# Loading a small vector to all 128 partitions by DMA instead of spreading it with a matrix product, and joining two runs of idle products

## The chip, the cores and the metric

The kernel runs on one core of one Trainium2 chip. The metric is the device time of one execution in microseconds (us). An execution is measured several times; most agree within 0.3%. "Span" below is the length of the profiled part of an execution, from the first to the last instruction of the program. In before it is about 1.8 us less than the time. Every run quoted here was classed as fast, and only such runs are compared.

## The reference, cut to what matters

Block-wise linear attention with a decay per head, followed by a gated feed-forward layer. Lambda is a vector of 8 values, one for each head, 32 bytes in all.

```python
# lam: [8] in 0.97..0.99; q, k, v: [4, 8, 768, 64]
Dmask = where(rel >= 0, lam ** rel, 0)            # inside a block
for b in range(nb):
    intra = (qb @ kb.T * Dmask) @ vb
    inter = (qb * lam ** (pos + 1)) @ kv_state
    out[b] = intra + inter
    kv_state = lam ** block * kv_state + (kb * lam ** (block - 1 - pos)).T @ vb
x = out as [3072, 512]
return (sigmoid(x @ w_gate) * (x @ w_val)) @ w_out
```

All powers of lambda are made on the chip. They are needed on every partition, so the 8 values have to get from one row in memory to 128 partitions.

Of the kernel before, what the change touches and what calls it, by code (L numbers as in the profile page):

```python
# [7 lines left out]
FP32 = mybir.dt.float32  # L8
BF16 = mybir.dt.bfloat16
AF = mybir.ActivationFunctionType  # L10
# [5 lines left out]
def kernel(  # L16
# [11 lines left out]
    nc = tc.nc  # L28

    B, H, S, D = q.shape  # L30
# [10 lines left out]
    const = ctx.enter_context(tc.tile_pool(name="const", bufs=1))  # L41
# [9 lines left out]
    ps_at = ctx.enter_context(tc.tile_pool(name="ps_at", bufs=5, space=bass.MemoryType.PSUM))  # L51
# [4 lines left out]


    lam_bc = const.tile([128, H], FP32, tag="lam_bc")
    lam1 = const.tile([1, H], FP32, tag="lam1")
    nc.sync.dma_start(out=lam1, in_=lam.partition_broadcast(1))  # L60

    WG = const.tile([128, NMT, DFF], BF16, tag="WG")
    WV = const.tile([128, NMT, DFF], BF16, tag="WV")
# [51 lines left out]
    jn = const.tile([128, 2], FP32, tag="jn")  # L115
    ip1 = const.tile([128, C], FP32, tag="ip1")
    tri = const.tile([128, C], FP32, tag="tri")
    ones = const.tile([1, 128], FP32, tag="ones")
    nc.vector.memset(zero, 0.0)
    nc.vector.memset(ones, 1.0)  # L120
    Sb = stp.tile([128, B, HP, D], BF16, tag="Sb", name="Sb")
    nc.vector.memset(ip1[:, 0:1], 1.0)
    w = 1
# [30 lines left out]
    def idle(n):  # L154
        for i in range(n):
            nc.tensor.matmul(wm, lhsT=zero[:, :C], rhs=zero, start=True, stop=True,
                             skip_group_check=True)

    idle(4)
    lamp = ps_at.tile([128, H], FP32, name="lamp", tag="ps")  # L160
    nc.tensor.matmul(lamp, lhsT=ones, rhs=lam1, start=True, stop=True)
    lnl = const.tile([128, H], FP32, tag="lnl")
    nc.scalar.activation(lnl, lamp, AF.Ln)
    lnp = const.tile([128, HP], FP32, tag="lnp")
    for u in range(2):
        us = slice(u * 64, (u + 1) * 64)
        nc.scalar.activation(lnp[us, :], lamp[us, u::2], AF.Ln)
    nc.scalar.copy(lam_bc, lamp)
    lamq0 = const.tile([128, HP, C], BF16, tag="lamq0")
    for hp in range(HP):  # L170
        nc.scalar.activation(lamq0[:, hp, :], ip1, AF.Exp, scale=lnp[:, hp:hp + 1])
# [6 lines left out]
    for u in range(2):  # L178
        us = slice(u * 64, (u + 1) * 64)
# [313 lines left out]
    load_gv(1, GW)  # L493
    load_gv(2, GW)

    idle(6)
    nc.vector.tensor_copy(Q[0][:, 0], q01[0])
    piece_tq0([0])
    make_mask(0)
# [198 lines left out]
```

## The kernel before: the parts that the change touches

The program is scheduled by hand: each engine's instructions are written in the order in which it is to execute them.

```python
lam_bc = const.tile([128, H], FP32, tag="lam_bc")
lam1 = const.tile([1, H], FP32, tag="lam1")
nc.sync.dma_start(out=lam1, in_=lam.partition_broadcast(1))      # 32 bytes, one partition
# ...
nc.scalar.dma_start(out=q01[0], ...)     # q of batch 0, f32, ScalarE's queue
nc.sync.dma_start(out=q01[1], ...)       # q of batch 1, f32, Sync's queue, behind lambda
# ... VectorE: zero, ones, ip1 (1..128), ident, tri, in about 20 small instructions
load(0, "k", 0, 2)                       # K of block 0, GpSimd's queue (casts f32 to bf16)
# ... the rest of q, v and the weights, GpSimd's queue

def idle(n):                             # products of zeros that nobody reads
    for i in range(n):
        nc.tensor.matmul(wm, lhsT=zero[:, :C], rhs=zero, ...)

idle(4)
lamp = ps_at.tile([128, H], FP32, name="lamp", tag="ps")
nc.tensor.matmul(lamp, lhsT=ones, rhs=lam1, start=True, stop=True)   # spread to 128 partitions
nc.scalar.activation(lnl, lamp, AF.Ln)
# ... Ln to lnp, copy to lam_bc; Exp to lamq0, pk, kds, dec;
#     between them ScalarE's cast of q01[1] to bf16
# ...
idle(6)
nc.vector.tensor_copy(Q[0][:, 0], q01[0])    # VectorE's cast of q of batch 0
piece_tq0([0])                               # first transposes on TensorE, q of batch 0
make_mask(0)
idle(1)
piece_tq0([1])                               # transposes of q of batch 1
piece_tk0(0)                                 # transposes of K, tile tk
# ... scores, masks, block 0's output, first products with the weights
make_lamq()                                  # VectorE, about 21 us: lp and lamq from lam_bc
# ... from about 25 us on: products with the weights, nearly without a gap
```

The idle products are there for the clock. In the trace of before TensorE runs at half rate up to 7.5 us: the transposes start 107 ns apart at 6.06 us and 56 ns apart at 7.93, an idle product lasts 634 ns before 7.2 us and 379 ns at 8.32, and the clock records have full rate from 7.72 us on.

## Time and profile before

| | before |
|---|---|
| time | 227.16 us median of 3 runs (227.02 to 227.65) |
| span of the profiled run | 225.7 us |
| TensorE busy | 217.9 us, 97% |
| K of block 0 landed | 7.82 us |
| first transposes of K | 7.86 us |
| steady products with the weights | from 25.9 us |

The page of the profile gives busy time by engine (us, share of the span, instructions) and the chain of work that ended last, as shares of the span. These are lines of the page of before:

```profile
PE 217.9 (97%) x1728; PEld 115.2 (51%) x1750; DVE 106.5 (47%) x194; ACT 79.1 (35%) x150; POOL 78.4 (35%) x77
...
PE 91%; DVE 3%; DMA 3%; issue 2%; ACT 1%; DVEq 0%; POOLq 0%
```

TensorE (PE) bounds the kernel as a whole. The change lies in the first 7 us, and there the chain is another. Below it stands in order of time for before, taken from the first 30 us: start, duration, what.

```profile
1.26 6.56 DMA kb<-in_k_dram
...
7.86 0.63 PE tk L242 x8
...
25.92 0.86 PE gp L419 x4
```

For 6.56 us the chain is one load, K's. Work that ends before 7.8 us has slack against it. The timeline of before shows that work: start, duration, engine, line of the program, operation, output and inputs, sizes, count, and in brackets the idle time before it with what ended that.

```profile
0.74 0.34 SPq L60 DMA_DIRECT2D lam<-in_lam_dram  x1
1.19 1.89 PE L156 MATMUL wm<-zero 128*128 128x512 bf16 x4 [1.19 <-DVE zero L119]
3.01 0.59 PE L161 MATMUL lamp<-lam,ones 1*128 1x8 f32 x2
...
3.64 0.18 ACT L163 ACTIVATE lnl<-lamp 128x8 f32<-128x8 f32 x1 [1.17 <-PE lamp L161]
4.25 1.28 ACT L171 ACTIVATE lamq<-ip,lnp 128x128 bf16<-128x128 f32 x4
5.47 0.41 DVE L497 CAST qb<-q0f 128x512 bf16<-128x512 f32 x1
5.63 0.60 ACT L174 CAST qb<-q1f 128x512 bf16<-128x512 f32 x1
6.06 0.63 PE L242 MATMUL tq<-ident,qb 128*128 128x128 bf16 x4
```

ScalarE (ACT) starts on lambda when the product lamp is there, works through lamq0 and then casts q of batch 1. VectorE (DVE) casts q of batch 0 at 5.47 us, and the first transposes follow at 6.06.

### The profile page before, as it was taken

How to read it: one execution, taken by the hardware profiler on the slowest of the kernel's cores; microseconds unless marked ns; L12 is line 12 of the kernel's file. 1: busy time of each engine (PE TensorE's matmuls, PEld its weight loads, DVE VectorE, ACT ScalarE, POOL GpSimd, SP SyncE). 2: the span in 40 equal slices, each digit the busy share in tenths (PEclk: the TensorE clock that was granted, in tenths of full speed). 3: DMA queues.
4: the chain of work that ended last, by engine and by line, in shares of the span. 5: the costliest groups of instructions: out<-in, count | busy, mean ns of one | idle time of the engine just before them, and what ended most of it. 6: DMA issues, size and time to landing. Idle time of an engine off the chain costs nothing.

```text
span 225.7 us, 4250 instructions
## 1 busy us (share of the span) xinstructions
PE 217.9 (97%) x1728; PEld 115.2 (51%) x1750; DVE 106.5 (47%) x194; ACT 79.1 (35%) x150; POOL 78.4 (35%) x77
## 2 busy tenths in 40 slices
PE   7789999999999999999999999999999999999994
PEld 2445454888864455444545444446444445444443
DVE  7798647586521622435742345742334840333300
ACT  5463234434422225333215333225333225333221
POOL 8987687973493007940005950000000000000000
PEclk9999999999999999999999999999999999999999
DMA  8999999999999991999521999921940012100022
GB/s 122 154 174 196 186 176 151 145 194 169 155 146 183 217 208 75 180 137 147 23 93 49 190 134 145 46 96 46 153 84 0 0 50 93 49 0 0 0 93 94
DMA packets 105749, 25.70 MB, mean 114 GB/s; under 512 B 95874, under 2 KB 102786, under 8 KB 105730
## 3 DMA queue, kind: packets, MB, share of 16 engines
q0 software_dynamic: 81264, 13.90, 94.6%
q1 hardware_dynamic: 23426, 11.28, 22.4%
q10 hardware_dynamic: 1040, 0.26, 0.5%
q8 instruction: 13, 0.21, 0.4%
q14 instruction: 6, 0.05, 0.1%
HBM read 28.31 MB, written 6.29 MB: 153 GB/s over the span
## 4 chain that ended last, share of the span: by engine, by line
PE 91%; DVE 3%; DMA 3%; issue 2%; ACT 1%; DVEq 0%; POOLq 0%
PE po L482 27%; PE gp L419 21%; PE vp L425 20%; PE gp L454 5%; PE vp L460 5%; PE sp L304 3%; PE gp L433 3%; PE op L316 3%; DMA kb<-in_k_dram 3%; PE op L328 1%; PE po L471 1%; PE cp L403 1%; DVE MT L206 1%; DVE lp L194 1%; DVE ht L446 1%
## 5 line engine op out<-in xcount | busy, mean ns | idle before, releaser
L428 DVE TENSOR_TENSOR ht<-sg,vp 128x512 bf16<-128x512 bf16 x54 | 37.2, 688 | 65.6 <-PE vp L425 60.4
L482 PE MATMUL po<-WO,ht 128*128 128x512 bf16 x266 | 61.3, 379 | 0.5
L419 PE MATMUL gp<-XT,WG 128*128 128x512 bf16 x211 | 55.0, 379 | 0.6 <-issue 0.2
L425 PE MATMUL vp<-XT,WV 128*128 128x512 bf16 x211 | 54.4, 379 | 0.0
L422 ACT ACTIVATE sg<-gp 128x512 bf16<-128x512 f32 x54 | 32.2, 597 | 59.3 <-PE gp L419 59.3
L482 PEld LDWEIGHTS <-ht 128*128 128x128 bf16 x276 | 26.2, 98 | 31.0
L425 PEld LDWEIGHTS <-WV 128*128 128x128 bf16 x216 | 21.1, 98 | 25.5
L419 PEld LDWEIGHTS <-WG 128*128 128x128 bf16 x216 | 20.8, 98 | 24.7
L485 ACT COPY ob<-po 128x512 f32<-128x512 f32 x23 | 13.5, 586 | 52.2 <-PE po L482 48.4
L208 DVE TENSOR_TENSOR MT<-sp,mask 128x512 bf16<-128x512 f32 x40 | 25.2, 683 | 9.3 <-PE sp L304 9.3
L386 POOL TENSOR_TENSOR sd<-Sb,dec 128x512 f32<-128x512 bf16 x8 | 8.1, 1036 | 42.7 <-DVE Sb L410 42.6
L454 PE MATMUL gp<-XT,WG 128*128 128x256 bf16 x96 | 14.4, 273 | 0.0
L460 PE MATMUL vp<-XT,WV 128*128 128x256 bf16 x96 | 14.4, 273 | 0.0
L464 DVE TENSOR_TENSOR ht<-sg,vp 128x256 bf16<-128x256 bf16 x24 | 10.0, 420 | 8.6 <-PE vp L460 8.6
L457 ACT ACTIVATE sg<-gp 128x256 bf16<-128x256 f32 x24 | 9.2, 384 | 13.0 <-PE gp L454 11.8
L92 POOL DMA_DIRECT2D vb<-in_v_dram x10 | 12.8, 1285 | 0.8 <-DMA WG<-in_moe_w_gate_dram 0.6
L377 POOL TENSOR_TENSOR kd<-kb,kds 128x1024 bf16<-128x1024 bf16 x6 | 11.3, 1905 | 4.5 <-DMA kb<-in_k_dram 4.5
L410 DVE TENSOR_TENSOR Sb<-cp,sd 128x512 bf16<-128x512 f32 x8 | 5.2, 686 | 15.5 <-PE cp L403 15.5
L343 ACT CAST XT<-op 128x512 bf16<-128x512 f32 x19 | 9.9, 598 | 2.1 <-PE op L316 2.0
L454 PEld LDWEIGHTS <-WG 128*128 128x128 bf16 x96 | 9.2, 98 | 1.7 <-issue 0.2
L460 PEld LDWEIGHTS <-WV 128*128 128x128 bf16 x96 | 9.4, 98 | 1.1
L78 POOL DMA_DIRECT2D qb<-in_q_dram x8 | 9.4, 1183 | 0.0
(84 smaller groups left out, 162.9 us busy)
## 6 DMA issues: line engine op xcount, KB each, us to landing
out_dram<-ob SPq DMA_DIRECT2D x21, 256.0 KB, 2.3
kb<-in_k_dram POOLq DMA_DIRECT2D x10, 256.0 KB, 11.4
qb<-in_q_dram POOLq DMA_DIRECT2D x8, 256.0 KB, 9.8
vb<-in_v_dram POOLq DMA_DIRECT2D x4, 512.0 KB, 14.9
WO<-in_moe_w_out_dram POOLq DMA_DIRECT2D x3, 512.0 KB, 9.0
WG<-in_moe_w_gate_dram POOLq DMA_DIRECT2D x5, 256.0 KB, 8.3
WV<-in_moe_w_val_dram POOLq DMA_DIRECT2D x5, 256.0 KB, 8.5
qb<-in_q_dram POOLq DMA_DIRECT2D x6, 128.0 KB, 8.6
```

Source lines behind the costliest of these rows:

```text
L92: nc.gpsimd.dma_start(out=lst[n][:, b0:b1], in_=src[b0:b1, :, sl, :].rearrange("b h s d -> s (b h) d"))
L208: nc.vector.tensor_tensor(out=out.rearrange("p (e x) c -> p e x c", e=2), in0=x.rearrange("p (e x) c -> p e x c", e=2), in1=mask.rearrange ...
L377: nc.gpsimd.tensor_tensor(out=KD[n][:, e], in0=K[n][:, e], in1=kds[:, e::2].unsqueeze(1).unsqueeze(3).to_broadcast([128, B, HP, D]), op=AL ...
L419: nc.tensor.matmul(gp, lhsT=WG[:, mt, fs], rhs=x[:, mt, :], start=(mt == 0), stop=(mt == NMT - 1))
L422: nc.scalar.activation(sg, gp, AF.Sigmoid)
L425: nc.tensor.matmul(vp, lhsT=WV[:, mt, fs], rhs=x[:, mt, :], start=(mt == 0), stop=(mt == NMT - 1))
L428: nc.vector.tensor_mul(HT[n, ft], sg, vp)
L454: nc.tensor.matmul(gp[:, cs], lhsT=WG[:, mt, fs], rhs=x[:, mt, cs], start=(mt == 0), stop=(mt == NMT - 1))
L460: nc.tensor.matmul(vp[:, cs], lhsT=WV[:, mt, fs], rhs=x[:, mt, cs], start=(mt == 0), stop=(mt == NMT - 1))
L464: nc.vector.tensor_mul(HT[n, ft][:, cs], sg[:, cs], vp[:, cs])
L482: nc.tensor.matmul(po, lhsT=HT[n, ft][:, tt * 128:(tt + 1) * 128], rhs=WO[:, ft, :], start=(ft == 0), stop=(ft == NFT - 1))
L485: nc.scalar.copy(ob, po)
```

## The change

The intent: the DMA writes lambda to all 128 partitions itself, so the product, its two operands and a copy go away, ScalarE need not wait for TensorE, and the idle products run without a break up to the first transpose.

```diff
     lam_bc = const.tile([128, H], FP32, tag="lam_bc")
-    lam1 = const.tile([1, H], FP32, tag="lam1")
-    nc.sync.dma_start(out=lam1, in_=lam.partition_broadcast(1))
+    nc.sync.dma_start(out=lam_bc, in_=lam.partition_broadcast(128))
 ...
-    ones = const.tile([1, 128], FP32, tag="ones")
     nc.vector.memset(zero, 0.0)
-    nc.vector.memset(ones, 1.0)
 ...
-    idle(4)
-    lamp = ps_at.tile([128, H], FP32, name="lamp", tag="ps")
-    nc.tensor.matmul(lamp, lhsT=ones, rhs=lam1, start=True, stop=True)
-    nc.scalar.activation(lnl, lamp, AF.Ln)
+    nc.scalar.activation(lnl, lam_bc, AF.Ln)
 ...
-        nc.scalar.activation(lnp[us, :], lamp[us, u::2], AF.Ln)
-    nc.scalar.copy(lam_bc, lamp)
+        nc.scalar.activation(lnp[us, :], lam_bc[us, u::2], AF.Ln)
 ...
-    idle(6)
+    idle(10)
     nc.vector.tensor_copy(Q[0][:, 0], q01[0])
```

## The prediction

> **What bounds the kernel now.** TensorE: the page's busy table gives PE 217.9 us of a 225.7 us span, and the chain that ended last is 91% PE. The change touches only the first 7 us. There the chain in order of time is not PE but the load of K for block 0: 6.56 us of "DMA kb" from 1.26, landed at 7.82; the transposes tk start at 7.86, then KS copies, scores and masks follow. Whatever ends before 7.8 us has slack.
>
> **What the change does.**
> - Lambda. Before, one 32-byte packet filled one partition, four idle products ran from 1.19 us, and the PE product lamp (two passes, 3.01 to 3.6) spread it; ScalarE's first Ln started at 3.64 (waits: on lamp). After, the load itself writes 128 partitions. In the DMA view of narrow windows Sync's two packets ran at 1.5 to 1.8 us, before those of q0f began at 1.83, so I expect lambda landed by 2.3 to 3.0 us. Ln can start at 2.6 to 3.1, behind the table load (ends 2.47): 0.5 to 1.0 us earlier. ScalarE's lamq0 needs ip1, which VectorE finishes at 3.93, so it moves only from 4.25 to about 3.9; the lam_bc copy (0.17 us) goes. ScalarE gains about 0.35 us.
> - VectorE. One memset goes, about 0.05 us. It stays busy until the q0 cast at 5.47 to 5.88, which releases the first transpose, so this stays at 5.9 to 6.1.
> - TensorE. Ten idle products in one run, 0.427 us from start to start: 1.19 to about 5.5, instead of ending at 6.1 with a 0.5 us pause for lamp. A gap of about 0.4 us appears before the first transpose.
> - DMA. 127 more packets. At 2.5 to 3.0 us the 16 engines moved 551 packets, so 127 cost about 0.12 us, partly hidden in idle time before 2.5 us. K's landing may move by 0 to 0.12 us, the only term on the critical path.
>
> **Clock.** Idle products last 634 ns before 7.2 us and 379 ns at 8.32, so TensorE reached full speed between, just as K landed. [...]
>
> **Sum.** Lambda path -0.35 us, off the chain; K's landing +0.1 us at most[...]. Predicted 227.1 us, 226.4 to 227.9 in 8 of 10. Faster by over 2%: 0.01; within 2%: 0.98; slower by over 2%: 0.01.
>
> **What would show it.** Ln waits for lambda's DMA and starts before 3.2 us; lamq0 ends near 5.2; ten idle products without a hole; first transpose within 0.15 us of 6.06; K landing within 0.15 us of 7.82; from tk on, the same timeline shifted by under 0.2 us.
>
> **What would make it wrong.** Lambda's packets queued behind q0f's, landing after 4.5 us, so that the second transposes pass 7.86; small packets delaying K by more than estimated[...].

The sum came to 227.1 us, with 226.4 to 227.9 as its range: the time of before, lambda's path off the chain, and at most 0.1 us for K's landing. It had a further term, for the clock.

## The result, and the profile after

| | before | after |
|---|---|---|
| time, median of 6 runs | 227.14 us (226.73 to 227.65) | 227.13 us (226.66 to 227.86) |
| ratio, 95% interval | | 0.9999 (0.9975 to 1.0023) |
| span of the profiled run | 225.7 us | 225.3 us |
| K landed | 7.82 us | 7.34 us |

A ratio here is the mean time of one kernel's fast runs over the mean of the other's fast runs of the same rounds, so it is not quite the ratio of the medians beside it.

The time did not change. The profile inside did. The same places in the timeline of after:

```profile
0.74 0.41 SPq L59 DMA_DIRECT2D lam_bc<-in_lam_dram  x1
1.19 3.84 PE L153 MATMUL wm<-zero 128*128 128x512 bf16 x10 [1.19 <-DVE ip L119]
3.84 0.21 ACT L157 ACTIVATE lnl<-lam_bc 128x8 f32<-128x8 f32 x1 [1.33 <-DMA lam_bc<-in_lam_dram]
4.39 1.28 ACT L164 ACTIVATE lamq<-ip,lnp 128x128 bf16<-128x128 f32 x4
4.97 0.76 DVE L490 CAST qb<-q0f 128x512 bf16<-128x512 f32 x1
5.79 0.40 PE L235 MATMUL tq<-ident,qb 128*128 128x128 bf16 x4 [0.76 <-DVE qb L490]
6.04 0.62 ACT L167 CAST qb<-q1f 128x512 bf16<-128x512 f32 x1 [0.19 <-DMA q1f<-in_q_dram]
6.71 0.40 PE L235 MATMUL tq<-ident,qb 128*128 128x128 bf16 x4 [0.31 <-ACT qb L167]
7.39 0.62 PE L235 MATMUL tk<-ident,kb 128*128 128x128 bf16 x8 [0.27 <-DMA kb<-in_k_dram]
```

Lambda came later, not earlier. ScalarE waited 1.33 us for the load and began Ln at 3.84 us, against 3.64 with the product. It then waited 0.19 us for q1f and cast it at 6.04 instead of 5.63 us. The second transposes waited for that cast, and K's transposes waited only 0.27 us more for K. So in this execution the change used up most of the slack.

Two lines of the DMA view of after, for 2.0 to 2.5 us, show how the loads were held up: queue, packets, MB, share of 16 engines. Queue q1 is Sync's (lambda, then q1f), q10 is ScalarE's (q0f).

```profile
q10 hardware_dynamic: 28, 0.01, 6.3%
q1 hardware_dynamic: 35, 0.00, 3.2%
```

In before the same half microsecond had this:

```profile
q10 hardware_dynamic: 287, 0.07, 63.1%
```

The packet records of the trace of after have lambda's 128 packets from 1.8 to 3.5 us, 13 ns apart (1.72 us over 128). Until q0f's packets began beside them at 2.34 us the 16 engines were nearly idle (3.1% busy from 1.8 to 2.34 us). In before, q0f's 1024 packets of 256 bytes ran from 1.84 to 3.36 us, 1.5 ns apart; in after they ran from 2.34 to 4.38, 2.0 ns apart.

The chain of after in order of time, beside that of before:

```profile
1.26 6.08 DMA kb<-in_k_dram
...
7.39 0.63 PE tk L235 x8
...
20.66 0.41 DVE lp L183
...
25.69 0.86 PE gp L412 x4
```

K's transposes are 0.47 us earlier (7.39 against 7.86), but the steady products only 0.23 us (25.69 against 25.92). Three questions follow. Was K's earlier landing due to the change? Where did the rest of that lead go? And is the equal time one of no effects, or of effects that cancel?

The runs answer a part of the third. In the 30 runs of after, e2, e3, e4 and e10 the time is 2.08 to 2.22 us above the span; in the 88 listed runs of before and of the other kernels it is 1.72 to 1.85. The traces have it behind the last instruction: the last semaphore update comes 2.26 us after the end of the span in after and 1.90 in before. So the changed kernel pays 0.37 us more after its own work is done, in every run, and the six spans of after are 225.0 us on average, about 0.4 less than in before (225.4, estimated as its mean time less 1.78). The equal time is these two together. What lengthens the closing was not tested: e1 has the load without it, and e7, e9 and e11 have the load and the joined idle run without it.

### The profile page after: what moved, and what is told of

Read it like the earlier page. It is cut to its first block, busy times and chain, and to the rows that moved or that the text cites. A ratio compares the mean times of both kernels' runs of the same rounds, so it can differ in the third digit from the quotient of the medians.

```text
span 225.3 us, 4243 instructions
## 1 busy us (share of the span) xinstructions
PE 216.0 (96%) x1726; PEld 114.3 (51%) x1748; DVE 106.8 (47%) x193; ACT 79.2 (35%) x149; POOL 78.5 (35%) x77
## 4 chain that ended last, share of the span: by engine, by line
PE 91%; DVE 3%; DMA 3%; issue 2%; ACT 1%; DVEq 0%; POOLq 0%
PE po L475 27%; PE gp L412 21%; PE vp L418 20%; PE gp L447 5%; PE vp L453 5%; PE sp L297 3%; PE gp L426 3%; PE op L309 3%; DMA kb<-in_k_dram 3%; PE op L321 1%; PE po L464 1%; PE cp L396 1%; DVE MT L199 1%; DVE lp L187 1%; DVE ht L439 1%
```

## The experiments

Theory A: everything in the changed part ends before K lands, so the change is worth nothing, and the differences between the two profiles are scatter. Theory B: the load costs 0.4 us or more and the unbroken idle run wins it back through the clock. Theories C and D, on K's landing, came later. Twelve kernels were run, in four calls; kernels of one call share a chip and the runs of before.

### e1_load_only: the load alone

The change without the joined idle run; the product stays as a dummy that waits for no load.

```diff
-    nc.sync.dma_start(out=lam1, in_=lam.partition_broadcast(1))
+    nc.sync.dma_start(out=lam_bc, in_=lam.partition_broadcast(128))
-    nc.tensor.matmul(lamp, lhsT=ones, rhs=lam1, start=True, stop=True)
+    nc.tensor.matmul(lamp, lhsT=ones, rhs=ones[:, :H], start=True, stop=True)
     # Ln reads lam_bc; the copy to lam_bc goes; idle(4) and idle(6) stay
```

> The load of lambda to 128 partitions alone: the idle products stay in two runs of 4 and 6, and the PE product lamp stays between them as a dummy (ones times ones) that waits for no load and that nobody reads. Theory A (slack): everything in the changed part ends before K lands, both halves of the change are worth nothing, ratio to before 0.998 to 1.002. Theory B (two effects cancel): the 128 packets delay the loads by 0.4 us or more and the unbroken idle run wins it back through an earlier clock; then this kernel, which has only the cost, is 0.4 us or more slower than before (ratio 1.002 or more), and its idle products are still at half rate (634 ns) at 6 us.

Measured: 226.82 us, ratio 0.9978 (0.9950 to 1.0006). Theory B fails: the kernel with only the supposed cost was not slower. K's transposes were at 7.40 us, as in after, and full rate came at 5.4 us by the clock records, so neither of theory B's signs was there.

### e2_after_again: the changed kernel, once more

> The changed kernel unaltered, for a second profile and a narrower interval. Theory A: ratio 0.999 to 1.001; lambda's Ln again at 3.6 to 4.0 us and q0's last packets again about 1 us later than in the first profile of before, since those follow from the number of packets; K's landing anywhere from 7.3 to 7.9 us, since I take the 0.48 us between the two first profiles for scatter. Theory B: K lands at 7.3 to 7.4 again and full clock comes at about 4.2 us again.

Measured: 226.89 us, ratio 0.9981 (0.9956 to 1.0005), which is e1's: the two forms of the idle run cannot be told apart by time. Theory A's 0.999 to 1.001 was missed by the point, not by the interval. Ln was at 3.85 us and the cast of q1 at 6.02, as in the first profile of after. Full clock came at about 7.2 us here by the clock records, against 4.3 in the first profile of after: it changes from execution to execution. Both intervals include 1. The spans tell more: 224.5 to 224.8 us here, 225.5 on average in the 11 runs of before beside it, a lead of 0.8 us of which 0.37 goes in the closing.

K landed at 7.30 us, but its transposes did not wait for it. At half rate the transposes of q still ran, and the chain leads back through them to VectorE's cast of q0, not to K:

```profile
6.83 0.48 PE tq L235 x4
...
7.35 0.64 PE tk L235 x8
```

So in this execution of the changed kernel, and likewise in e3's, the slack was gone. In the second profile of before (before_again below), with K at 7.21 us, the chain leads through the idle products too. How much slack there is depends on when K lands and on the clock before that.

### e3_no_idle_run: no idle run at all

```diff
-    idle(10)
```

> The changed kernel without the run of ten idle products before the first transpose; the later single ones stay. Theory A and B agree that the array is then at half rate when K lands: tk's 8 transposes take about 1.0 us instead of 0.62, scores and first products twice as long[...]. I expect +0.6 to +2 us (ratio 1.003 to 1.009). If it is not slower (below 1.001), the clock before 12 us is worth nothing here and no part of theory B about the clock can hold.

Measured: 227.24 us, ratio 0.9997 (0.9973 to 1.0022). The chain in order of time:

```profile
7.34 1.05 PE tk L235 x8
...
20.03 5.30 PE gp L426 x24
25.33 0.86 PE gp L412 x4
```

K's transposes took 1.05 us instead of 0.63 as expected, but the rest of the forecast missed: the scores at 8.90 us already ran at full rate (8 products in 0.44 us), and the steady products came 0.24 us after e2's (25.33 against 25.09). I had expected 0.6 to 2 us; how long the half rate would last was not shown. The idle run was worth about 0.4 us here (0.9997 against 0.9981), with intervals of 0.5 us and more on each ratio.

### e4_lambda_x4: four times the load

```diff
+    for i in range(3):
+        lamx = const.tile([128, H], FP32, tag=f"lamx{i}", name=f"lamx{i}")
+        nc.sync.dma_start(out=lamx, in_=lam.partition_broadcast(128))
```

> The changed kernel with four such loads of lambda on Sync's queue, 512 packets of 32 bytes, three of them to tiles that nobody reads: the suspected cost of the load four times. In the first profile of after, one load delayed q1f's landing so that ScalarE's cast of q1 started at 6.04 instead of 5.63 us, 0.3 us before it would hold up K's transposes. Theory A: each further load delays q1f by about 0.4 to 0.9 us, so the cast starts at 7.2 to 8.7 us, and tk's transposes at 8.5 to 9.8 us instead of 7.4; time +0.8 to +2.0 us (ratio 1.0035 to 1.009). If the packets cost nothing, ratio within 0.002 of 1.

Measured: 233.24 us, ratio 1.0274 (1.0243 to 1.0306), about 6.2 us. The sign was right and the size was missed by three to eight times. The chain in order of time:

```profile
2.61 8.82 DMA q1f<-in_q_dram
11.45 0.63 ACT qb L170
...
12.73 0.87 PE tk L238 x8
```

q1f stood behind 512 small packets that came out from 1.8 to 8.2 us, again 13 ns apart. K's transposes came 5.3 us later than in after (12.73 against 7.39). The rest went to the clock: all six runs had a mean granted clock of 0.971 to 0.985. So each such load costs the queue about 1.6 us (6.5 us over four). Against the 0.27 us of slack left in after, a second load would not fit; that is an estimate from this rate, not a run.

### before_again: the null test

> The kernel before against itself: a null test of the timing and a second profile. Ratio 0.999 to 1.001. In the first profile of before, K landed at 7.82 us and the first semaphore writes of K's 16 engines were spread from 5.6 to about 7.4 us; in the four profiles with lambda's 128-packet load K landed at 7.34 to 7.40. Theory C (the small packets, by holding back q0 and q1, let the 16 engines work on K in step, so that K lands 0.45 us earlier): K lands at 7.7 to 7.9 again. Theory A (scatter): K lands anywhere from 7.3 to 7.9, with no preference for 7.8.

Measured: ratio 0.9996 (0.9981 to 1.0011). K landed at 7.21 us and its transposes were at 7.26, where the first profile of before had 7.82 and 7.86. So before also has early landings; theory C fails. Its times lay between 226.32 and 227.31.

### e5_lamp_after_run: lambda 2 us late

```diff
-    idle(4)
+    idle(10)
     lamp = ...
-    idle(6)
```

> The kernel before with all ten idle products ahead of the PE product lamp: lambda reaches ScalarE about 2.5 us later (Ln at 6.0 to 6.2 instead of 3.64 us; earlier, 5.0 to 5.5, if full clock comes early). This measures the slack of lambda's path. ScalarE's cast of q1 then starts at about 8.0 to 8.3 us instead of 5.63, and K's transposes, which follow q1's on TensorE, at 8.8 to 9.2 instead of 7.86: about 1.2 us past the slack. I expect +0.5 to +1.3 us (ratio 1.002 to 1.006). If the ratio is within 0.001 of 1, lambda's path has over 2.5 us of slack and its route was never able to matter.

Measured: 228.52 us, ratio 1.0074 (1.0055 to 1.0092). Ln started at 5.70 us, 2.06 later than in before, and the steady products at 26.92, 1.0 later. K's transposes came at 8.95, 1.1 later than in before. So lambda's path had about 1 us of slack against K's late landing there, and the other 1.1 us reached the transposes. The forecast in time, up to 1.006, was passed: the remaining part went to the clock, and every run had a mean granted clock of 0.985 or 0.992.

### e6_before_plus_load: the packets alone

```diff
     nc.sync.dma_start(out=lam1, in_=lam.partition_broadcast(1))
+    lamx = const.tile([128, H], FP32, tag="lamx", name="lamx")
+    nc.sync.dma_start(out=lamx, in_=lam.partition_broadcast(128))
```

> The kernel before with a second load of lambda, to 128 partitions of a tile that nobody reads, between its own load and q1's on Sync's queue: the packets alone, with lambda still spread by the PE product and the idle products in two runs. Theory C: q0's and q1's last packets 0.8 to 1.0 us later, K landing at 7.3 to 7.45 us as in the four profiles with such a load, and the time 0.1 to 0.6 us below before (ratio 0.9975 to 0.9995). Theory A: K anywhere from 7.3 to 7.9, ratio 0.999 to 1.001. If the packets cost (theory B): K later than 7.9, ratio over 1.001.

Measured: 228.30 us, ratio 1.0055 (1.0043 to 1.0067). The time does not answer the question, but the trace does: K landed at 7.79 us, not at 7.3 to 7.45, so the packets did not bring K forward in this build, and theory C fails here too. Its premise failed in part: q1f's last packet came 1.7 us later than in before, but q0f's only 0.04 (3.40 against 3.36), although this load, issued 0.4 us behind q0f's, put as many small packets beside it.

As to the time, TensorE's last product and VectorE's last copy ended within 0.02 us of those of before; the extra came behind them. The timelines of the end, first of e6, then of before:

```profile
222.53 1.22 SPq L479 DMA_DIRECT2D out_dram<-ob  x2
```

```profile
222.55 0.82 SPq L477 DMA_DIRECT2D out_dram<-ob  x2
```

The last two output loads took 0.4 us longer to issue, and the program ended 3.8 us after VectorE started its last copy instead of 3.0 (span 226.5 against 225.7). The semaphore records of the two traces differ there: in before, the closing row of waits on Sync has the semaphores of the last two output loads at its end; in e6 the last output load has one that is second in the row, and seven further waits, about 0.06 us each, follow its landing. That the added DMA moved the later ones to other semaphores, and so made the end longer, is my reading; no run tested it. An added DMA was not a clean experiment here.

### e7_after_lamq_act: the chain at 20 us moved to ScalarE

Where did the lead go? In the timeline of after, lines of VectorE and GpSimd between 19.5 and 26 us:

```profile
20.23 0.87 POOL L85 DMA_DIRECT2D qb<-in_q_dram  x1 [0.23 <-DMA WV<-in_moe_w_val_dram]
20.58 0.68 DVE L183 COPY lp<-lam_bc 64x4 f32<-64x4 f32 x2
...
22.93 0.87 POOL L85 DMA_DIRECT2D kb<-in_k_dram  x1 [0.48 <-DMA WV<-in_moe_w_val_dram]
...
23.17 0.85 DVE L190 CAST lamq<-lp 128x512 bf16<-128x512 f32 x1
...
24.67 1.02 PE L426 MATMUL gp<-XT,WV 128*128 128x512 bf16 x4 [0.61 <-DVE ht L439]
```

The same stretch of e2, which is the same program:

```profile
20.55 0.34 DVE L183 COPY lp<-lam_bc 64x4 f32<-64x4 f32 x2
...
21.00 0.87 POOL L85 DMA_DIRECT2D qb<-in_q_dram  x1 [0.41 <-DMA WV<-in_moe_w_val_dram]
...
22.80 0.63 DVE L190 CAST lamq<-lp 128x512 bf16<-128x512 f32 x1
...
24.07 1.02 PE L426 MATMUL gp<-XT,WV 128*128 128x512 bf16 x4
```

Two tiny copies took 0.68 us when GpSimd (POOL) was in the middle of issuing a DMA, and 0.34 when it was not. In after, the first of them ended at 21.07 (the chain: 20.66 plus 0.41) and GpSimd's issue at 21.10 (20.23 plus 0.87). The cast took 0.85 against 0.63, and 0.43 in e3, where 0.06 us of an issue ran beside it. The copies in the other profiles fit: 0.60 us in before_again and 0.59 in e1, which began in the middle of an issue, and 0.33 to 0.34 in before, e3, e5 and e6, where 0.11 us of an issue at most ran beside them. Why they are slower beside an issue was not shown. GpSimd's issues in these lines waited for landings of earlier loads (0.23, 0.48 and 0.41 us), so their times were set by the DMA stream and not by TensorE. VectorE came to the copies at the same time in both (20.58 and 20.55 us); what differed was the issue (20.23 against 21.00). That is where a lead went.

```diff
+    # two Ln to lnq, as lnp but in lamq's order
+    def exp_lamq(ks):
+        for i in ks:
+            nc.scalar.activation(lamq[:, i, :], ip1, AF.Exp, scale=lnq[:, i:i + 1])
+    exp_lamq((0, 1))      # in ScalarE's idle time, before K's copies
 ...
+    exp_lamq((2, 3))      # behind them
 ...
-    make_lamq()
```

> The changed kernel with lamq made by ScalarE (two Ln, four Exp, in its idle time before 10 us) instead of by VectorE's 10 instructions between 20.6 and 24 us, where in the traces the lead of 0.67 us that after had over before at 20 us shrank to 0.23 at 25 us and TensorE waited 0.2 to 0.6 us for VectorE's product ht. If that wait is what gives the early lead back: TensorE runs through from 17.9 to 25 us without a gap, its products after 25 us start 0.3 to 0.8 us earlier than in after, and the time is 0.3 to 0.8 us below after (ratio to before 0.995 to 0.998). If not, ratio as for after, 0.998 to 1.000.

Measured: 227.05 us, ratio 1.0001 (0.9989 to 1.0013), correct. The gap did go:

```profile
1.26 6.67 DMA kb<-in_k_dram
...
7.98 0.63 PE tk L233 x8
...
20.32 5.29 PE gp L424 x24
25.60 0.86 PE gp L410 x4
```

From K's transposes to the steady products took 17.62 us (25.60 less 7.98), against 18.30 in after and 18.06 in before. This edit takes VectorE's whole chain away, not the collision alone; in e2, where the chain met the issues less, the stretch took 17.74. So the collision cost about 0.6 us in after (18.30 less 17.74). The time is not better because K landed at 7.93 us in this build, 0.6 us later than in after. The forecast in time missed, and it opened the question of what moves K.

### e8_before_lamq_act and e9_after_lamq_again: both sides without the collision

e8 is before with the edit of e7; e9 is e7 unaltered, on the same chip as e8.

> The kernel before with lamq made by ScalarE in its idle time before 10 us, as in e7_after_lamq_act: VectorE's chain that ran into GpSimd's DMA issues at 20 to 24 us is gone on the side of before too. From K's transposes to the products at 25 us, the profiles took 17.6 us where that chain was absent or undisturbed and up to 18.4 us where it ran into them. Theory A: with the collision gone on both sides the change is still worth nothing: this kernel and e9_after_lamq_again within 0.15% of each other, and in both the products at 25 us start 17.6 us (plus or minus 0.15) after K's transposes. If the change has a real gain that the collision hid, this kernel is 0.2% or more slower than e9_after_lamq_again.

> e7_after_lamq_act unaltered, beside its counterpart on the same chip, with a second profile. In e7's profile K's transposes started late (7.98 us) and its five times lay within 0.25 us. If K's landing is scatter between runs, this profile may have them at 7.3 us, and then a span near 224.6 us (7.35 plus 17.6 plus the 199.6 us that every profile but one needed after 25 us); if it belongs to this build, 7.9 to 8.0 again and a span of 225.2. Theory A: ratio to e8_before_lamq_act 0.9985 to 1.0015.

Measured: e8 226.78 us, ratio 0.9996 (0.9982 to 1.0010), five times within 0.22 us. e9 227.10 us, ratio 1.0024 (1.0005 to 1.0044). They differ by 0.28%, more than theory A allowed and in the direction that the change costs. K landed at 7.44 us in e8 and at 7.96 in e9. From K's transposes to the steady products e8 took 17.78 us. The chain of e9:

```profile
1.26 6.70 DMA kb<-in_k_dram
...
8.01 1.05 PE tk L233 x8
...
26.68 0.86 PE gp L410 x4
```

In two of e9's six runs, of which this is one, the mean granted clock was 0.985; they took 228.12 and 228.13 us, the other four 227.05 to 227.10. With these four alone e9 is 0.13% above e8, inside what theory A allowed: half of the difference is the lost clock. K's transposes took 1.05 us, at half rate. The clock records of this profile have full rate from 4.3 to 7.7 us and half rate from there to 14.6: it came early and was lost just before K.

The traces show what goes with keeping it. Take the 3.41 us that follow the start of full rate and count TensorE's busy time in them; 3.41 us is the length of the half-rate stretch in the clock records of e10, and that of e9 is twice as long. It was 1.90 us or more in the eight profiles that kept the full rate (2.07 in after, 2.50 in e2, 1.90 in e11, 2.28 or more in the others), and 1.75 or less in the four that lost it (1.75 in e10, 1.74 in e9, 1.50 in e4, 1.35 in e5); e3 and e7 have no clock records. In after and e9 full rate came at about the same time (4.28 and 4.32 us); K's transposes began inside that stretch in after (7.39) and behind it in e9 (8.01). My reading, from these twelve profiles alone: full rate was kept where TensorE was busy for 1.90 us or more of that stretch, and in e9 a late K took some of that work away. No run was made to test it.

### e10_after_pad32 and e11_after_lamq_pad32: nothing but placement

K landed at 7.30 to 7.35 us in after, e1, e2 and e3, and at about 7.95 in both profiles of e7's build. The packet records say that this is not the transfer: in e2 and e7 the last of the 16 closing packets of K's load began at 7.00 and 7.02 us, but the last semaphore update followed 0.30 us later in one and 0.91 in the other. Theory D was that the address of K's tile matters: the change takes away two small tiles, and everything behind them in SBUF moves.

```diff
     mask = const.tile([128, H, C], FP32, tag="mask")
+    pad = const.tile([128, 8], FP32, tag="pad", name="pad")      # never used
```

> The changed kernel with 32 unused bytes per partition behind its constants: no instruction is added, only the tiles of q, k, v and everything behind them move by 32 bytes in SBUF. In the built programs, K's first tile starts at a multiple of 64 bytes in after, e1, e2, e3 and e8, where K landed at 7.3 to 7.45 us, and at 32 past such a multiple in before, e7 and e9 (the change took away two small tiles, so it moved this), where K landed at 7.82, about 7.2, 7.93 and 7.96. Theory D (placement): a start 32 bytes off delays the landing of K; here, off by 32 as in before, K lands at 7.7 to 8.0 us and the time is 0.2 to 0.6 us above e2_after_again's 226.89, ratio to before 0.9995 to 1.002. Theory A (scatter): K at 7.3 to 7.4 as in the other profiles of the changed kernel, ratio 0.998 to 0.9995.

> e9_after_lamq_again with the same 32 unused bytes, which bring K's tile from 32 past a multiple of 64 bytes back onto one: lamq made by ScalarE, lambda by the wide load. Theory D: K lands at 7.3 to 7.45 us instead of 7.93 and 7.96, the products at 25 us start 17.6 us after K's transposes, span about 224.6 us and time about 226.4: 0.5 to 0.9 us below e7 and e9 (227.05, 227.10), ratio to before 0.996 to 0.9985, the fastest version of this study if so. Theory A: 227.0 as e7 and e9, K at 7.9.

Measured: e10 228.00 us, ratio 1.0046 (1.0030 to 1.0062). e11 227.07 us, ratio 1.0003 (0.9991 to 1.0015). The chains, e10 first:

```profile
1.26 6.75 DMA kb<-in_k_dram
...
8.06 0.75 PE tk L236 x8
```

```profile
1.26 6.75 DMA kb<-in_k_dram
...
8.06 0.64 PE tk L234 x8
```

e10 has the instructions of the changed kernel and ran on the chip with the number that e2's had, yet K landed 0.67 us later than in after (8.01 against 7.34). In the two of its six runs with the clock at 1.0, it took 227.61 and 227.65 us; in the other four, at 0.992, it took 227.72 to 228.50. So this build, with an unused tile of 32 bytes, lost more against before than anything the change did (1.0046, where e2 had 0.9981). Before's own two profiles have K 0.6 us apart with no edit at all, so one profile of one padded build does not show that the 32 bytes moved K. And e11 refutes theory D: there the padding brought K's tile onto a multiple of 64 bytes, and K still landed at 8.01.

One pattern fits every profile of a kernel with one 128-partition load in place of the product, but I found it afterwards and no run tested it: K's tile starts at a multiple of 128 bytes in after, e1, e2 and e3 (K at 7.30 to 7.35 us), and 32 or 64 past one in e7, e9, e10 and e11 (7.93 to 8.01). With lambda's narrow load, before (32 past) had 7.82 and 7.21 and e8 (64 past) 7.44, so there the pattern does not decide. What sets K's landing stays open.

### What the profiles have in common

| profile | K's transposes | steady products from | span less that |
|---|---|---|---|
| before | 7.86 | 25.92 | 199.8 |
| after | 7.39 | 25.69 | 199.6 |
| before_again | 7.26 | 25.62 | 199.7 |
| e1 | 7.40 | 25.62 | 199.6 |
| e2 | 7.35 | 25.09 | 199.6 |
| e3 | 7.34 | 25.33 | 199.6 |
| e4 | 12.73 | 32.45 | 199.9 |
| e5 | 8.95 | 26.92 | 199.8 |
| e7 | 7.98 | 25.60 | 199.6 |
| e8 | 7.49 | 25.27 | 199.7 |
| e9 | 8.01 | 26.68 | 199.6 |
| e10 | 8.06 | 25.91 | 199.7 |
| e11 | 8.06 | 25.69 | 199.6 |

The last column is the span less the column before it. It hardly moves, so whatever the spans of these kernels differ by is decided before the steady products: by K's landing, by the clock behind it, by the collision at 20 to 24 us and, in e4 and e5, by the delays put in. e6, whose end was 0.8 us longer, is the exception and is left out. The 0.37 us of the closing comes on top, outside the span. No version beat both kernels clear of noise. The best median, e8's 226.78 us, has an interval that includes 1.

## Why the prediction was right

The predicted time, 227.1 us, was measured as 227.13, and the class was right. The main step held for the profiled execution: the change lies before K lands, and the profile of after still has K's load at the head of its chain (e2's has not, and there nothing was left of the slack). e1 and e2 show no difference in time clear of noise, for the load alone and for the whole change; the joined idle run alone was not run. That the number fits to 0.03 us is luck: the span fell by about 0.4 us and the closing behind it grew by 0.37, and the prediction had neither. Several of the smaller steps were wrong and did not show in the total.

- "I expect lambda landed by 2.3 to 3.0 us. Ln can start at 2.6 to 3.1": wrong. Ln started at 3.84 us, behind the load. The mis-sized term is "127 cost about 0.12 us". It took the rate of q0f's 256-byte packets for the small ones; they came 13 ns apart and took 1.7 us.
- "ScalarE gains about 0.35 us": wrong in sign. lamq0 started 0.14 us later (4.39 against 4.25), and the cast of q1 0.41 us later, because q1f stood behind lambda's packets. In e4, with 512 packets before it, q1f's load was at the head of the chain (its cast at 11.45 us).
- "First transpose within 0.15 us of 6.06": it came at 5.79. VectorE's cast started 0.5 us earlier but took 0.76 us instead of 0.41; it had no effect.
- "K landing within 0.15 us of 7.82": it came at 7.34. The packets are neither needed for it nor enough: before's own second profile had 7.21 without them and e6 7.79 with them. The cause stays open.
- "From tk on, the same timeline shifted by under 0.2 us": it was shifted by 0.47 us at tk and 0.23 at 25 us. Part of the lead was given back to the collision with GpSimd, which I had not seen.
- The clock: a late or lost full rate was among the risks. The risk was real. The unbroken run brought full rate early in after (4.28 us, against 7.72 in before), and its idle products then ended early, at 5.03 us. In the twelve profiles full rate was lost with TensorE busy for 1.75 us or less in the 3.41 us that followed, and kept with 1.90 or more, as worked out under e9. Of 34 runs of kernels with the unbroken run (after, e2, e7, e9, e10, e11), 8 had a mean clock of 0.992 or below; of 66 with the run in two parts (before 44, before_again, e1, e6, e8), one did. In e4 and e5, also with ten idle products in one run, the work was delayed on purpose and all 12 runs had lost it. A half-rate stretch of 3.41 us cost about 0.6 us on average in e10, and one of twice that length 1.05 us in e9. For the changed kernel itself it was 1 run of 12, so it stayed small. K came late in most of the other builds, and as after and e9 show, that is part of the same picture; no run separated the two.

So the equal time is not one of no effects. The load took most or all of its own slack. The span shrank by about 0.4 us while K landed 0.48 us earlier in the profile, which is open as to its cause; the closing behind the span took 0.37 us back, and its cause is open too. What remains between builds and runs, some 0.5 us, goes with K's landing, the clock behind it and the collision at 20 us.

## What to carry to other kernels

A change off the critical path is worth nothing in time, but it can spend the slack that protected it; read what is left of that slack afterwards (here 0.3 us in one execution and nothing in another), not only the total. Compare the spans as well as the times: here they disagreed by 0.37 us. Here a load of 32 bytes to 128 partitions was 128 packets that took 1.7 us for 4 KB, and the load behind it in the queue came later (q1f's last packet at 5.35 us against 4.44), so put such a load behind what is urgent (not run here), or spread the values by an engine that is idle anyway, as before did. And before an effect of a few tenths of a per cent is put down to a change, move the tiles by a few bytes without changing an instruction: here one such build differed by half a per cent.
